# An S4 layer beside a feed-forward on Trainium2: the input transform's stores put on ScalarE's queue, and the last second weight loaded into the buffer of the raw first weights

## The chip, the cores and the metric

The kernel runs on one core of one Trainium2 chip. The metric is the device time of one execution in microseconds (us), lower is better. Three runs of the kernel before give a median of 1121.8.

## The reference, cut to what matters

The input is one sequence of L = 2048 rows with D = 576 channels. It is normalised row by row; the normalised rows go through a state-space layer (S4, a long convolution for each channel) and, in parallel, through a feed-forward with 4608 hidden features; both results are added to the input. Everything is float32.

```python
K = einsum("dn,dnl,dn->dl", C, exp(dt * A * l), dt * B).real    # N = 128 states, l < 2048
y = irfft(rfft(pad(xn)) * rfft(pad(K)))[:2048] + xn * Dskip     # per channel
h = silu(xn @ w1)                                               # 576 -> 4608
return x + y + h @ w2                                           # 4608 -> 576
```

## The kernel before

**Number format.** TensorE is fed in its faster float32 form (fp32r). To keep the precision, every operand is split into a high part and a low part, and every product becomes three matmuls: high by high, high by low, low by high. In names, `h` and `l` at the end mean these parts (`gh`, `gl`; `yh`, `yl`).

**The feed-forward** (`ffn`, `wino_ffn`) carries the program. The 4608 hidden features are 36 tiles of 128 (`NFT`), in blocks of four (`FT`, so `NCH` = 9 blocks). The tokens go in two halves of 1024. For a hidden tile there is a *first weight* (576 x 128 of `w1`) and a *second weight* (128 x 576 of `w2`). In the first half, raw second weights (`w2r`) come in on SyncE's queue (SP) at line 275, ScalarE and VectorE split them (L284), and the split form is also stored to a scratch `dw2` in device memory. In the second half from hidden tile 8 on, a scheme with seven products instead of eight for 2 x 2 blocks of the first product is used (`wino_ffn`). It runs in units n = 4 to 17, of two hidden tiles each, 2n and 2n + 1. A unit needs:

- raw first weights, `load_w1` (SP, tag `w1r`): one tile of 128 x 5 x 256 values for a unit. There are two such buffers, one in the pool `wp` and one in `w1x`, used by units in turn. `prep` then forms the splits and sums of them on ScalarE and VectorE (the last one of a unit's is on L371 in the profile), after which the raw buffer is not read again.
- second weights, already split: `second(n, i)` loads tile 2n + i from `dw2` on GpSimd's queue (POOL, L480) into a ring of five buffers (tag `w2`). It is called from `side_w(3)`, once in each unit, for tile 1 of this unit and tile 0 of the next one. A load can start only when TensorE has read the tile that held the buffer five loads ago for the last time. Tile 35 is the last of all.

The second product is `down`: for each block of 128 tokens and each half of the channels, TensorE sums 24 matmuls or fewer into `po` (L328), and VectorE adds that to the running sum `acc` (L333). The activations are `gf` (silu, on ScalarE, L306), `gh` (L307) and `gl` (VectorE, L308).

**The state-space layer** runs between the steps of the feed-forward. `weave` interleaves the two when the program is written; its tail comes last:

1. `spread`, the input transform: it loads rows of the normalised input (`xr`), splits them (`sp`, L149), TensorE multiplies them with a matrix `s1` into `pu`, ScalarE copies both channel halves to the tile `u1` (L156), and `u1` is stored to the scratch `d1u` (L157). There are 32 such stores of 288 KB, and one buffer `u1` (`u` in the profile). So the next copy has to wait until the store before it has landed.
2. `kgen`, beside it, makes the kernel K with sines on ScalarE and products on VectorE; TensorE sums `z` (L880) from `kt`, and 18 stores of 512 KB take it to the scratch `d1k`, on GpSimd's queue as well (L893), two at a time.
3. `spectral`: 32 steps. SP loads a row block of `d1u` and of `d1k`, TensorE multiplies both with matrices `m` that GpSimd loads (L902), and the product goes back through L997 (`pb`) and ScalarE (`yo`) to the scratch `d2` (GpSimd).
4. the output transform: SP loads `ys` from `d2` (L1004), six row blocks ahead, two DMAs each; `conv` multiplies pairs of them (`py`, L1016). For eight of the sixteen row blocks ScalarE copies the result to `yt` and GpSimd adds it into the output (L172, `out_dram<-yt`, accumulating stores); for the other eight `down` adds the feed-forward's last sum onto it, at the end.

**What sets the order.** The program is built with a scheduler that takes all instructions with their dependencies and a model of their times, and writes one list for each engine (`schedule_with_timeline_sim=True`). Blocks under `high_priority` go first where they can; `behind` keeps an instruction from being put ahead of a given one. So an edit in one place can move instructions elsewhere. [...]

Of the kernel before, what the change touches and what calls it, by code (L numbers as in the profile page):

```python
# [11 lines left out]
F32R = mybir.dt.float32r  # L12
# [5 lines left out]
P = 128  # L18
L = 2048
D = 576  # L20
# [5 lines left out]
NFT = FF // P  # L26
# [15 lines left out]
def kernel(  # L42
# [21 lines left out]
    nc = tc.nc  # L64
    FT = 4
# [38 lines left out]
    wp = ctx.enter_context(tc.tile_pool(name="wp", bufs=2))  # L104
# [33 lines left out]
    def spread(up):  # L138

        s1 = up.tile([P, 2, P], F32R, name="s1", bufs=1)  # L140
        nc.gpsimd.dma_start(s1, cs1)
        for j in range(NJ):
            src = up.tile([P, D], F32, tag="xr", name="xr")
            nc.sync.dma_start(src, dxn[:, j])
            for m in range(2):
                lo, hi = slice(64 * m, 64 * m + 64), slice(64 - 64 * m, 128 - 64 * m)
                u1 = up.tile([P, D], F32, tag="u1", name="u1")
                sp = up.tile([P, D], F32R, tag="sp", name="sp")
                nc.scalar.copy(sp[lo, :], src[lo, :])  # L149
                nc.vector.tensor_sub(sp[hi, :], src[lo, :], sp[lo, :])  # L150
                for h in range(2):
                    hs = slice(h * HD, (h + 1) * HD)
                    pu = pss.tile([P, 512], F32, tag="pss", name="pu")
                    nc.tensor.matmul(pu[:, :HD], s1[:, 0, :], sp[:, hs], start=True, stop=False)
                    nc.tensor.matmul(pu[:, :HD], s1[:, 1, :], sp[:, hs], start=False, stop=True)
                    nc.scalar.copy(u1[:, hs], pu[:, :HD])  # L156
                nc.gpsimd.dma_start(  # L157
                    d1u.rearrange("(p m j) d -> m j p d", m=2, j=NJ)[m, j], u1)
                yield j

# [275 lines left out]
    def wino_ffn(load_w1, prep, WT, first, end, W2, before, down):  # L436

        ps_a = ps1.tile([P, 512], F32, tag="ps1", name="pa")
        ps_c = ps1.tile([P, 512], F32, tag="ps1", name="pc")
        A, A22, S1, S2, S3, S4, x40, x41, d4 = wino["x"]  # L440
        nc.tensor.matmul(ps_a, x40[:, :P], x40, start=True, stop=True)
        G = {}

        def unit(name, n, a):
            h, l = WT[name, n]
            return h[:, a:a + 2], l[:, a:a + 2]

        def prod(dst, w, x, start=False, stop=False):
            (wh, wl), (xh, xl) = w, x
            n = 0  # L450
            for a, v in ((wh, xh), (wh, xl), (wl, xh)):
                for kt in range(2):
                    pins["pe"] = nc.tensor.matmul(dst, a[:, kt], v[:, kt], start=start and n == 0, stop=stop and n == 5,  # L453
                                                  skip_group_check=True).ins
                    n += 1

        def rest(dst, name, n, at, x4, stop=True):
            for i in range(2):
                pins["pe"] = nc.tensor.matmul(dst, WT[name, n][i][:, at], x4, start=False, stop=stop and i == 1,  # L459
                                              skip_group_check=True).ins  # L460

        def gate(src, b, f):
            gf = gp.tile([P, 512], F32, tag="gf", name="gf", bufs=2)
            spare = len(G) % 6 == 5
            gh, gl = ((wino["pool"] if spare else gp).tile([P, 512], F32R, tag=n, name=n) for n in ("gh", "gl"))
            G[b, f] = gh, gl
            with tc.high_priority():
                nc.scalar.activation(gf, src, AF.Silu)
                pins["gh"] = nc.scalar.copy(gh, gf).ins  # L469
                pins["gl"] = nc.vector.tensor_sub(gl, gf, gh).ins  # L470

        def load(n):
            if n < end:
                load_w1(1, n // 2, n % 2 * 2)

        def second(n, i):
            if n < end:
                f = 2 * n + i
                w = wp.tile([P, 2, D], F32R, tag="w2", name="w2", bufs=FT + 1)
                pins["load"] = nc.gpsimd.dma_start(w, dw2[f - WINO_C * FT]).ins  # L480
                W2[1, f // FT, f % FT] = w

        load(first + 1)
        second(first, 0)

        def downs(n):

            if n < first:
                return [lambda jj=jj: down(before, jj) for jj in range(4)]
            b = 1 - n % 2  # L490
            if n == first:
                ns = (n,)
            else:
                ns = (n - 1, n)
            return run_of(b, ns)

        def run_of(b, ns):
            fs = [2 * n + i for n in ns for i in range(2)]
            blk = (1, NCH - 1 if ns[-1] == end - 1 else WINO_C, b)
            return [lambda jj=jj: down(blk, jj, [(G[b, f], W2[1, f // FT, f % FT]) for f in fs]) for jj in range(4)]  # L500

        for n in range(first, end):
            load(n + 2)
            d = downs(n - 1)
            pb = ps2.tile([P, 512], F32, tag="ps2", name="pb2")
            f5 = wino["pool"].tile([P, 512], F32, tag="f5", name="f5", bufs=1)
            units = {k: unit(*k) for k in (("c1", n, 0), ("c1", n, 2), ("t13", n, 0), ("t13", n, 2),
                                           ("t24", n, 0), ("t24", n, 2), ("c2", n, 0))}

            def p1():  # L510
                prod(pb, units["c1", n, 0], A[0], start=True)
                with tc.high_priority():
                    nc.scalar.copy(ps_a, pb)

            def p5():
                prod(ps_c, units["t13", n, 0], S1, start=True)
                rest(ps_c, "c2", n, 2, x41)
                with tc.high_priority():
                    nc.scalar.copy(f5, ps_c)

            def p6():
                prod(pb, units["t24", n, 0], S2)
                with tc.high_priority():
                    nc.vector.tensor_add(ps_c, pb, f5)

            def p7():
                prod(pb, units["t13", n, 2], S3)
                with tc.high_priority():
                    nc.vector.tensor_add(f5, pb, f5)

            def c11():
                prod(ps_a, units["c1", n, 2], A[1])
                rest(ps_a, "c1", n, 4, x40)
                gate(ps_a, 1, 2 * n)

            def c12():
                prod(ps_c, units["c2", n, 0], S4)
                rest(ps_c, "c2", n, 2, d4)
                gate(ps_c, 1, 2 * n + 1)

            def c2x():
                gate(f5, 0, 2 * n + 1)
                prod(pb, units["t24", n, 2], A22)
                gate(pb, 0, 2 * n)

            def c1x():
                c12()
                c11()

            def side_w(k):  # L550
                if k == 1:
                    prep(n + 1, "c2")
                elif k == 2:
                    prep(n + 1, "c1")
                    prep(n + 1, "sums")
                elif k == 3:
                    second(n, 1)
                    second(n + 1, 0)

            if n == first:  # L560
                order = ((p1, 0), (c11, 1), (2,), (p5, p6, 3), (p7,))
                ends = c12, c2x
            else:
                order = ((p1, p5), (0,), (p6, 1), (p7, 2), (3,))
                ends = (c1x, c2x) if n % 2 == 0 else (c2x, c1x)
            for steps in order:
                for f in steps:
                    if callable(f):
                        f()
                    else:  # L570
                        d[f]()
                        side_w(f)
                yield 0
            rest(pb, "c1", n, 4, x41, stop=False)
            for k, f in enumerate(ends):
                f()
                prep(n + 1, ("t13", "t24")[k])
                yield 0
        b = 1 - (end - 1) % 2
        for f in run_of(b, (end - 2, end - 1)):  # L580
            f()
            yield 0
        for k, f in enumerate(run_of(1 - b, (end - 1,))):
            f()
            if k % 2:
                yield 0
# [579 lines left out]
```

## Time and profile before

| | before |
|---|---|
| median of three runs | 1121.8 us (1121.65 to 1125.08) |
| the profiled execution's own time | 1124.72 us |
| its span, first to last instruction | 1123.0 us |
| granted TensorE clock, mean | 0.995 |
| TensorE (PE) busy | 1094.8 us, 97% |
| VectorE (DVE) busy | 939.7 us, 84% |
| ScalarE (ACT) busy | 737.7 us, 66% |
| GpSimd (POOL) busy | 170.1 us, 15% |
| moved by DMA | 173.68 MB, mean 155 GB/s |

All moments and durations below are of the one profiled execution and are counted from the start of its span. A row of instructions reads: start, duration, engine, line, operation, result <- operands, shape, count, and in brackets the idle time of the engine ahead of it with what ended that. A row of waits reads: engine, tile and line, <- what released it: total, count, longest. A row of a window (A:B) reads: its length, then busy time and count of PE, PEld (weight loads), DVE, ACT, POOL, then the granted clock, the share of the DMA engines, and GB/s. A row of DMA issues gives the size of each transfer and the us from issue to landing. Buffer numbers are left out of names unless a text says otherwise.

### The profile page before, as it was taken

What the parts mean: (1) busy time and instruction counts of PE and PEld (TensorE: products, weight loads), DVE (VectorE), ACT (ScalarE), POOL (GpSimd) and SP (SyncE); (2) the same over time, 40 slices, a digit from 0 to 9 for tenths busy, and PEclk for the clock granted to TensorE, in tenths of its full rate; (3) what the DMA queues carried; (4) which work ended last, traced back from release to release, by engine and by line L of the source; (5) the groups of instructions that cost most, each with busy time, mean ns of one, the idle gap of its engine ahead of it and who ended that gap; (6) DMA issues with size and microseconds to landing.
All of it is one profiled execution on the core that took longest, in us unless ns stands there. A gap on an engine that the chain in (4) does not pass through costs nothing.

```text
span 1123.0 us, 23098 instructions
## 1 busy us (share of the span) xinstructions
PE 1094.8 (97%) x9101; PEld 988.9 (88%) x9101; DVE 939.7 (84%) x1597; ACT 737.7 (66%) x1321; POOL 170.1 (15%) x262
## 2 busy tenths in 40 slices
PE   6999899999899999999999999999999999999997
PEld 5998789898788889898899898999999999999786
DVE  6699888899899999989999978989888788886322
ACT  4665556777676767766776646877778787875320
POOL 1022100101010101010522012112111211210220
PEclk9999989999999999999999999999999999999999
DMA  9456532525344444447773334555555655554994
GB/s 271 141 163 202 163 121 70 160 82 157 122 126 121 139 152 124 157 92 251 231 192 101 95 71 142 188 174 153 171 177 175 178 164 158 175 158 114 230 222 104
DMA packets 90445, 173.68 MB, mean 155 GB/s; under 512 B 14768, under 2 KB 53696, under 8 KB 89696
## 3 DMA queue, kind: packets, MB, share of 16 engines
q1 hardware_dynamic: 63184, 97.32, 29.3%
q0 software_dynamic: 26480, 73.11, 23.4%
q10 hardware_dynamic: 672, 1.77, 0.7%
q8 instruction: 72, 1.18, 0.4%
q14 instruction: 37, 0.30, 0.1%
HBM read 109.64 MB, written 62.60 MB: 153 GB/s over the span
## 4 chain that ended last, share of the span: by engine, by line
PE 78%; DVE 6%; DMA 6%; issue 4%; ACT 3%; POOL 1%; SPq 0%; POOLq 0%; DVEq 0%; ACTq 0%
PE po L328 34%; PE ph L298 15%; PE pb L453 7%; PE pc L453 3%; PE kp L865 2%; PE pb L997 2%; PE pu L997 2%; PE pk L997 2%; DMA d1u<-u 2%; PE pa L453 2%; PE ph L300 1%; PE ph L299 1%; PE z L880 1%; PE pc L459 1%; DMA w1r<-in_B_w_dram 1%
## 5 line engine op out<-in xcount | busy, mean ns | idle before, releaser
L328 PE MATMUL po<-w,gh 128*128 128x288 f32 x2304 | 477.2, 297 | 8.2 <-DVE acc L333 3.2
L328 PEld LDWEIGHTS po<-w,gh 128*128 128x128 f32 x2304 | 375.8, 188 | 25.5 <-issue 6.0
L328 PE MATMUL po<-w,gl 128*128 128x288 f32 x1152 | 334.8, 296 | 0.6 <-DVE gl L308 0.6
L328 PEld LDWEIGHTS po<-w,gl 128*128 128x128 f32 x1152 | 215.5, 188 | 3.0 <-DVE gl L308 0.9
L333 DVE TENSOR_TENSOR acc<-po,acc 128x288 f32<-128x288 f32 x296 | 129.5, 450 | 65.8 <-PE po L328 64.6
L298 PE MATMUL ph<-xh,w1h 128*128 128x512 f32 (+1 forms) x368 | 100.3, 391 | 2.4 <-ACT w1h L266 1.3
L298 PE MATMUL ph<-xl,w1h 128*128 128x512 f32 (+1 forms) x368 | 100.4, 387 | 0.0
L298 PE MATMUL ph<-xh,w1l 128*128 128x512 f32 (+1 forms) x368 | 98.1, 383 | 0.0
L306 ACT ACTIVATE gf<-ph 128x512 f32<-128x512 f32 (+1 forms) x92 | 53.2, 578 | 51.0 <-PE ph L300 35.8
L298 PEld LDWEIGHTS ph<-xl,w1h 128*128 128x128 f32 x368 | 67.4, 192 | 12.1
L298 PEld LDWEIGHTS ph<-xh,w1h 128*128 128x128 f32 x368 | 66.4, 194 | 13.1 <-ACT w1h L266 1.6
L298 PEld LDWEIGHTS ph<-xh,w1l 128*128 128x128 f32 x368 | 66.2, 188 | 11.6
L902 POOL DMA_DIRECT2D m<-in_cm_dram x64 | 33.9, 532 | 216.2 <-PE pu L997 135.4
L308 DVE TENSOR_TENSOR gl<-gf,gh 128x512 fp32r<-128x512 f32 (+1 forms) x92 | 60.7, 661 | 4.0 <-ACT gh L307 3.8
L826 ACT ACTIVATE c<-th 128x1040 f32<-128x1040 f32 x36 | 38.7, 1074 | 36.2 <-DVE th L825 36.1
L307 ACT CAST gh<-gf 128x512 fp32r<-128x512 f32 (+1 forms) x92 | 55.4, 604 | 8.2 <-PE po L328 6.8
L157 POOL DMA_DIRECT2D d1u<-u x32 | 17.8, 557 | 275.4 <-ACT u L156 275.4
L824 ACT ACTIVATE c<-th,magic 128x1040 f32<-128x1040 f32 x36 | 42.0, 1166 | 23.7 <-DVE C L845 19.3
L470 DVE TENSOR_TENSOR gl<-gf,gh 128x512 fp32r<-128x512 f32 x56 | 37.8, 688 | 20.7 <-ACT gh L469 20.3
L844 DVE TENSOR_TENSOR S<-th,C 128x1024 f32<-128x1024 f32 x36 | 43.9, 1220 | 13.4 <-ACT th L827 13.3
L893 POOL DMA_DIRECT2D d1k<-stage x18 | 29.6, 1647 | 151.8 <-ACT u L156 99.9
L825 DVE SCALAR_TENSOR_TENSOR th<-c,th 128x1040 f32<-128x1040 f32 x36 | 44.4, 1234 | 3.1 <-ACT c L824 3.0
(273 smaller groups left out, 2419.3 us busy)
## 6 DMA issues: line engine op xcount, KB each, us to landing
w1r<-in_B_w_dram SPq DMA_DIRECT2D x35, 512.0 KB, 4.0
dw<-w SPq DMA_DIRECT2D x28, 576.0 KB, 4.2
w<-dw POOLq DMA_DIRECT2D x28, 576.0 KB, 5.5
w2r<-in_B_w_dram SPq DMA_DIRECT2D x44, 288.0 KB, 5.0
d1u<-u POOLq DMA_DIRECT2D x32, 288.0 KB, 3.7
d1k<-stage POOLq DMA_DIRECT2D x18, 512.0 KB, 8.7
ul<-d1u SPq DMA_DIRECT2D x32, 288.0 KB, 2.9
kl<-d1k SPq DMA_DIRECT2D x32, 288.0 KB, 3.6
```

The source lines that it names most:

```text
L298: nc.tensor.matmul(ph, w[:, kt, :], v[:, kt, a:e], start=n + kt == 0, stop=False)
L306: nc.scalar.activation(gf, ph, AF.Silu)
L307: pins["gh"] = nc.scalar.copy(gh, gf).ins
L308: pins["gl"] = nc.vector.tensor_sub(gl, gf, gh).ins
L328: pins["pe"] = nc.tensor.matmul(po[:, :HD], gs[g][:, js], ws[:, w, hs], start=n == 0 and j not in begun, stop=n == 3 * len(terms) - 1, ski ...
L333: nc.vector.tensor_add(acc[j][:, hs], po[:, :HD], acc[j][:, hs])
L453: pins["pe"] = nc.tensor.matmul(dst, a[:, kt], v[:, kt], start=start and n == 0, stop=stop and n == 5, skip_group_check=True).ins
L824: nc.scalar.activation(c65, th, AF.Identity, bias=magic)
L825: nc.vector.scalar_tensor_tensor(th, c65, MAGIC, th, op0=ALU.subtract, op1=ALU.subtract)
L826: nc.scalar.activation(c65, th, AF.Abs)
L844: nc.vector.tensor_mul(ov3, t[:, :, 0:64].rearrange("n d (x y) -> n d x y", y=32), mv3)
L997: nc.tensor.matmul(dst, st, mv[:, hs], start=n == 0, stop=n == 3 * len(terms) - 1)
```

## The change

Two edits.

*First*, `spread` issues its 32 stores of `u1` with `nc.scalar.dma_start` instead of `nc.gpsimd.dma_start`. Data, size, buffer and destination stay.

*Second*, the load of the last second weight, tile 35 of 36 (f = `NFT` - 1), no longer takes a buffer of the ring `w2`. It goes into the buffer that held the raw first weights of an even unit (tag `w1r` in `wp`; 10 x 128 of its values, of which 2 x 576 are used). Unit 16 is the last to use that buffer for raw weights. The call comes at `side_w(3)` of unit 16 (`n == end - 2`) instead of unit 17, right after those for tiles 33 and 34. The call of unit 17 then finds tile 35 in the table `W2` and does nothing. GpSimd still issues it.

```diff
@@ spread
-                nc.gpsimd.dma_start(
+                nc.scalar.dma_start(
                     d1u.rearrange("(p m j) d -> m j p d", m=2, j=NJ)[m, j], u1)
@@ wino_ffn
         def second(n, i):
-            if n < end:
-                f = 2 * n + i
-                w = wp.tile([P, 2, D], F32R, tag="w2", name="w2", bufs=FT + 1)
+            f = 2 * n + i
+            if n < end and (1, f // FT, f % FT) not in W2:
+                if f == NFT - 1:
+                    w = wp.tile([P, 10 * P], F32R, tag="w1r", name="w2", bufs=1)
+                    w = w[:, :2 * D].rearrange("p (k d) -> p k d", k=2)
+                else:
+                    w = wp.tile([P, 2, D], F32R, tag="w2", name="w2", bufs=FT + 1)
                 pins["load"] = nc.gpsimd.dma_start(w, dw2[f - WINO_C * FT]).ins
                 W2[1, f // FT, f % FT] = w
@@ side_w
                 elif k == 3:
                     second(n, 1)
                     second(n + 1, 0)
+                    if n == end - 2:
+                        second(n + 1, 1)
```

The edit adds six lines, so a line number of the program before that lies behind `second` is six higher in the program after (L997 becomes L1003); `second`'s own DMA goes from L480 to L484.

**GpSimd, the last second weights.** This is the end of GpSimd's list before, from the last stores of the spectral step on. The names `w_...` are second weights: w_12839 is tile 31, w_12841 tile 32, w_13125 tile 33, w_13127 tile 34, and w_13399 tile 35.

```order
L952 DMA d_59<-yo 128x576 x3
L480 DMA w_12839<-dw_63 128x1152
L480 DMA w_12841<-dw_63 128x1152
L172 DMA out_dram<-yt 32x1152 x8
L480 DMA w_13125<-dw_63 128x1152
L480 DMA w_13127<-dw_63 128x1152
L172 DMA out_dram<-yt 32x1152 x8
L480 DMA w_13399<-dw_63 128x1152
```

And after, where tile 35 is w_13129:

```order
L958 DMA d_59<-yo 128x576 x3
L484 DMA w_12839<-dw_63 128x1152
L484 DMA w_12841<-dw_63 128x1152
L484 DMA w_13129<-dw_63 128x1152
L172 DMA out_dram<-yt 32x1152 x8
L484 DMA w_13125<-dw_63 128x1152
L172 DMA out_dram<-yt 32x1152 x4
L484 DMA w_13127<-dw_63 128x1152
L172 DMA out_dram<-yt 32x1152 x4
```

Tile 35 has moved from the end to right behind tile 32, ahead of all the accumulating stores, and four of these stores now stand between tiles 33 and 34.

**TensorE, the last product of the spectral step.** The place is the second product of unit 15's activations, whose first reader of second weight 31 is still to come; m_12092 is the last matrix of the spectral step, and w_12086, w_12381, w_12383 and w_12601 are second weights 26 to 29. Before:

```order
L328 MATMUL po<-w_12383,gl 128x288
L997 MATMUL pb<-yh,m_12092 128x288 x2
L328 MATMUL po<-w_12601,gh 128x288 x2
L997 MATMUL pb<-yl,m_12092 128x288
L997 MATMUL pb<-yh,m_12092 128x288
L997 MATMUL pb<-yl,m_12092 128x288
L997 MATMUL pb<-yh,m_12092 128x288
L328 MATMUL po<-w_12601,gl 128x288
L328 MATMUL po<-w_12086,gh 128x288 x2
```

After:

```order
L328 MATMUL po<-w_12086,gh 128x288 x2
L328 MATMUL po<-w_12086,gl 128x288
L328 MATMUL po<-w_12381,gh 128x288
L1003 MATMUL pb<-yh,m_12092 128x288 x2
L328 MATMUL po<-w_12381,gh 128x288
L328 MATMUL po<-w_12381,gl 128x288
L1003 MATMUL pb<-yl,m_12092 128x288
L1003 MATMUL pb<-yh,m_12092 128x288
L1003 MATMUL pb<-yl,m_12092 128x288
L1003 MATMUL pb<-yh,m_12092 128x288
L328 MATMUL po<-w_12383,gh 128x288 x2
L328 MATMUL po<-w_12383,gl 128x288
```

The six matmuls of the product have moved back against the second product: behind their last one, 40 matmuls followed before up to the last one that reads w_12086, and 9 follow now. The buffer of w_12086 (tile 26) is the one that tile 31 goes to.

**ScalarE, one of the 32 stores.** The place is in the input transform, at the tile u_3100, whose store goes out right behind a pair of `d1k` stores. The names c and th are tiles of the sines, and w_3225 is a split second weight. Before:

```order
L824 ACTIVATE c_3327<-th,magic 128x1040
L156 COPY u_3100<-pu 128x288
L149 CAST sp<-xr 64x576
L284 CAST w_3225<-w2r 128x576
L306 ACTIVATE gf<-ph 128x512
L826 ACTIVATE c_3327<-th 128x1040
L827 ACTIVATE th<-th 128x1040
L828 ACTIVATE c_3327<-c_3327,halfpi 128x1040
L306 ACTIVATE gf<-ph 128x512
L156 COPY u_3212<-pu 128x288 x2
```

After:

```order
L830 ACTIVATE c_3327<-th,magic 128x1040
L156 COPY u_3100<-pu 128x288
L149 CAST sp<-xr 64x576
L284 CAST w_3225<-w2r 128x576
L157 DMA d1u<-u_3100 128x576
L306 ACTIVATE gf<-ph 128x512
L832 ACTIVATE c_3327<-th 128x1040
L833 ACTIVATE th<-th 128x1040
L834 ACTIVATE c_3327<-c_3327,halfpi 128x1040
L306 ACTIVATE gf<-ph 128x512
L156 COPY u_3212<-pu 128x288 x2
```

The store does not stand directly behind the copy that it waits for, but two casts later; behind it come a `gf` and two sines, and then the copy of the next tile into the same buffer.

## The prediction

> **What bounds the kernel now.** I read the page's busy times and chain, then TensorE's waits, then the windows in which they fall.
>
> ```profile
> PE 1094.8 (97%) x9101; PEld 988.9 (88%) x9101; DVE 939.7 (84%) x1597; ACT 737.7 (66%) x1321; POOL 170.1 (15%) x262
> PE 78%; DVE 6%; DMA 6%; issue 4%; ACT 3%; POOL 1%; SPq 0%; POOLq 0%; DVEq 0%; ACTq 0%
> PE pt L122 <- DVE xn L190: 8.9, 1, 8.9
> PE po L328 <- DVE acc L333: 3.2, 2, 2.0
> PE z L880 <- ACT kt L872: 2.2, 3, 1.2
> PE po L328 <- DMA w<-dw: 2.0, 1, 2.0
> 280.80:308.80 28.00, 24.80 (x279) 22.35 (x279) 24.65 (x37) 17.33 (x29) 1.64 (x3) 1.00 0.38 122
> 1038.80:1066.80 28.00, 28.00 (x228) 22.08 (x228) 10.81 (x22) 10.78 (x25) 8.39 (x12) 1.00 1.00 230
> ```
>
> TensorE is busy for 97% of the span, and 78% of the chain that ended last lies on it. The change removes no matmul, so it can win only TensorE's idle time, or time at a low clock. The first wait (8.9 us) is the load at the start, which the change leaves alone. Two others are within its reach: the one for a second weight (2.0), and the idle 3.2 us (28.00 less 24.80) from 280.8 on. From 1038.8 on the DMA engines are full (share 1.00, 230 GB/s) while TensorE never idles: a later transfer is felt there only where it has no slack.
>
> **Part one of the change: the last second weight.** The rows are GpSimd's loads of second weights (w<-dw) and one of its stores, the last load's flight, TensorE around it, and the window behind it (the column 0.50 is the granted clock).
>
> ```profile
> 1033.33 1.09 POOL L480 DMA_DIRECT2D w<-dw  x2 [5.42 <-PE po L328]
> 1062.20 2.27 POOL L480 DMA_DIRECT2D w<-dw  x2
> 1065.90 3.16 POOL L172 DMA_DIRECT2D out_dram<-yt  x4 [1.43 <-ACT yt L966]
> 1090.24 8.11 DMA w<-dw
> 1096.16 0.29 PE L328 MATMUL po<-w,gh 128*128 128x288 f32 x1
> 1098.49 0.51 PE L328 MATMUL po<-w,gh 128*128 128x288 f32 x2 [2.04 <-DMA w<-dw]
> 1077.01 3.18 PE po L328 x24
> 1098.90:1102.30 3.40, 3.40 (x24) 2.89 (x30) 1.77 (x4) 0.00 (x0) 0.00 (x0) 0.50 0.00 1
> 1037.81 1.15 DVE L371 TENSOR_TENSOR w1l<-w1r,w1h 128x512 fp32r<-128x512 f32 x2
> ```
>
> Load 35 goes out at 1090.24, when TensorE has let go of its buffer, and flies 8.11 us. Between the matmuls at 1096.16 and 1098.49 lie 2.33 us, where such matmuls follow each other every 0.13 (3.18 for 24): **2.2 us** lost. Behind it the clock is half for 3.40 us: another **1.7 us**.
>
> In the new order load 35 stands right behind load 32. It waits for the last reading of unit 16's raw weights, by 1037.81 plus 1.15, and is needed 59 us later: even the longest flight here leaves it far ahead. Both terms go. What is late next? Load 34 now stands behind four stores (a row of four takes 3.16 us from 1065.90), so it leaves at about 1069 instead of 1063; its first use is beside load 35's, near 1093, so 24 us are left, and it costs nothing.
>
> The price lies elsewhere. The scheduler has also moved the last product of the spectral step, whose stored result SP waits for before it loads ys for the output transform:
>
> ```profile
> 1026.27 0.29 PE L997 MATMUL pb<-yh,m 128*128 128x288 f32 x1
> 1029.98 18.99 SPq L1004 DMA_DIRECT2D ys<-d  x16
> 1043.32 1.20 PE L1016 MATMUL py<-ys,s 64*32 64x288 f32 x24
> w<-dw POOLq DMA_DIRECT2D x2, 576.0 KB, 9.8
> ys<-d SPq DMA_DIRECT2D x1, 288.0 KB, 12.4
> w<-dw POOLq DMA_DIRECT2D x1, 576.0 KB, 9.6
> 1071.84 0.50 PE L328 MATMUL po<-w,gh 128*128 128x288 f32 x2
> ```
>
> (The three DMA rows are the windows 1033.3 to 1033.9, twice, and 1062.1 to 1062.5; last column: us to landing.) Before, that product ran at 1026.27. By the new order only 9 matmuls lie between it and the last reading of second weight 26, which releases load 31 at 1033.3; so it runs about 1.2 us (9 x 0.13) before that, near 1031.6: 5.3 later, and ys starts near 1035.3. The first py product stands where it stood, at 1043.3. It now has 8 us for the four ys loads of its pair. At 230 GB/s a ys load (288 KB) takes 1.3 us and a second weight 2.6, and loads 31 and 32 now lead: 2 x 2.6 + 4 x 1.3 = 10.4 us of transfers from 1033.3, ending at 1043.7, plus a flight of some 2. The ends are no wait and 5.2 (both weights wholly in front, nothing overlapped); I take **+1.0**, since the first product needs only half of the pair.
>
> Load 33 is next. It left at 1062.20, landed 9.6 later at 1071.8, and TensorE used it at 1071.84: no slack. The train of loads before it now begins 3.3 us later (1033.3, not 1030.0) and is longer by load 35's 2.6: up to 5.9 late. Against that, GpSimd's loads overtake SP's here (9.8 beside 12.4 for issues in the same 0.6 us), so the delay falls mostly on ys loads with time to spare. I take 0 for load 33; 5.9 is a rival's.
>
> **Part two: 32 stores from GpSimd's queue to ScalarE's.** ScalarE's waits for these stores, the worst of them, SP's issues beside it, and what TensorE lost:
>
> ```profile
> ACT u L156 <- DMA d1u<-u: 14.1, 6, 4.8
> 275.01 12.28 DMA d1u<-u
> 275.18 0.68 ACT L284 CAST w<-w2r 128x576 fp32r<-128x576 f32 x1
> 277.59 0.60 ACT L306 ACTIVATE gf<-ph 128x512 f32<-128x512 f32 x1 [1.73 <-PE ph L300]
> 287.37 0.70 ACT L156 COPY u<-pu 128x288 f32<-128x288 f32 x2 [4.83 <-DMA d1u<-u]
> 293.18 1.16 PE L880 MATMUL z<-f,kt 64*128 64x128 f32 x16 [1.24 <-ACT kt L872]
> 301.79 0.53 PE L328 MATMUL po<-w,gh 128*128 128x288 f32 x2 [1.96 <-DVE acc L333]
> 275.47 1.38 SPq L275 DMA_DIRECT2D w2r<-in_B_w_dram  x1
> 280.96 2.28 SPq L275 DMA_DIRECT2D w2r<-in_B_w_dram  x1
> w2r<-in_B_w_dram SPq DMA_DIRECT2D x1, 288.0 KB, 11.5
> w2r<-in_B_w_dram SPq DMA_DIRECT2D x1, 288.0 KB, 3.6
> L165 ACTq DMA_DIRECT2D acc<-in_A_u_dram x4: 370/438/443, 0.7 to 2.1; - x4
> L893 POOL DMA_DIRECT2D d1k<-stage x18 | 29.6, 1647 | 151.8 <-ACT u L156 99.9
> ```
>
> (The two w2r rows with KB are the loads of 275.47 and 331.43.) Two large stores d1k (18 in all, so 9 bursts) go out at 271.5 and 273.1; the d1u store behind them takes 12.28 us, so ScalarE cannot refill the single buffer u and waits 4.83. TensorE then idles 1.24 and 1.96, 3.2 us for 4.83: 0.66 per us.
>
> *What a new queue wins.* In the new order the store stands behind the cast of w, so it leaves near 275.9. A transfer of the same 288 KB on SP's queue at 275.47 took 11.5 us; so the store lands near 287.4, where it landed at 287.3. Gain 0. The other end is the load of 331.43, half a us into its burst: 3.6 us, and the whole 3.2 us are won. I take 0, as 275.47 is the nearer row. [...]
>
> *What the issue costs.* ScalarE's four own DMA issues took 0.44 us. 32 x 0.44 = 14 us, but each stands behind a cast of 0.6 us or longer, under which it can run, and ScalarE is 66% busy. In a burst an issue can stick: 1.38 and 2.28 us on SP. Queued behind it are gf (for TensorE's next products) and the two sines that VectorE waits for. Ends: 0, if the idle 1.73 us that follow at 277.59 cover it, and 9 x 2.28 x 0.66 = 13.6 us. I take one burst without that cover, 1.38 x 0.66 = **+0.9**. GpSimd loses its 32 issues, which no row here waits for.
>
> **The sum.** -2.2 - 1.7 + 1.0 + 0 + 0.9 = -2.0 us on a span of 1123.0 (an execution of 1124.7). That execution is 2.9 us above the median of the runs; the difference is put on the median: 1121.8 - 2.0 = **1119.8**. A measurement of this kernel can tell about 0.3%, 3.4 us, from no change.
>
> **Rivals.**
> *The stores land early and the wait at the end goes*: -3.9 - 3.2 = -7.1, 1114.7; without the new ys wait and issue cost but with no gain on the stores, -3.9, 1117.9. For it: 3.6 us at 331.43. Against: 11.5 at 275.47. [...] Chance 0.30.
> *Load 33 comes late* (slower): 5.9 us of wait and a half clock of 1.7 again: -2.0 + 5.9 + 1.7 = +5.6, 1127.4. For it: no slack at 1071.84, DMA share 1.00. Against: GpSimd's loads overtake. It decides from a wait of 3.7 us. Chance 0.17.
> *ScalarE sticks in its issues* (slower): +13.6 for +0.9 gives +10.7, 1132.5; it decides from 9.5 us of blocking, 1.06 per burst (6.3 / 0.66). In the new order 19 of the 32 stores also wait for a counter shared with SP's transfers, which adds to it. Against: the idle time behind the issue. Chance 0.13.
> *It does nothing*: something else holds TensorE at 1096. Against: the row names the load alone. 1121.8, chance 0.02.
>
> **The numbers.** Forecast 0.38 (its own range 1118.4 to 1123.0). Faster by over 0.3%: 0.30. Within: 0.38 + 0.02 = 0.40. Slower: 0.17 + 0.13 = 0.30. The range 1114.0 to 1129.0 holds the first rival and the second, and leaves out most of the third and a little below the first.
>
> **What would show it.** Right: no wait of po on w<-dw near 1096, no half clock behind it; ScalarE still waits about 14 us on d1u; ys starts near 1035; py waits 0 to 2 us. Wrong: ScalarE's waits on d1u near 0 (first rival); po waiting on w<-dw near 1071 (second); DMA issues over 1 us on ScalarE and more waits on acc and kt (third).

## The result and the profile after

The changed kernel takes **1119.67 us** (median of 14 runs, 1116.19 to 1121.6); the kernel before, run 14 times in turn with it, takes 1122.73 (1119.62 to 1127.89). The ratio is 0.9966, with a 95% interval of 0.9952 to 0.998: 3.8 us of 1122.7, just past the 0.3% that can be told. The forecast was 1119.8, 2.0 us faster and within 0.3%. The number came out near, but the parts of the sum did not; they are taken apart below. One of the twelve executions of experiment 3 took 1190.6 us, where the others took 1115.6 to 1120.07, and is left out of its ratio.

The page of the profiled execution after (1118.54 us, span 1116.8):

```profile
PE 1091.8 (98%) x9101; PEld 987.3 (88%) x9101; DVE 940.6 (84%) x1597; ACT 737.0 (66%) x1321; POOL 152.6 (14%) x230
```

The same number of matmuls in 6.2 us less of span. That is more than the runs give: this execution lies 1.1 us below its kernel's median, and the profiled one of before 2.0 above its own. So single profiles place a change here, but do not size it.

**Part one, the load of tile 35.** GpSimd's loads of tiles 35, 33 and 34 in the timeline after, and the first products with tiles 33 and 35:

```profile
1035.36 0.53 POOL L484 DMA_DIRECT2D w<-dw  x1 [4.33 <-DVE w1l L371]
1060.73 0.59 POOL L484 DMA_DIRECT2D w<-dw  x1 [2.26 <-PE po L328]
1064.65 0.59 POOL L484 DMA_DIRECT2D w<-dw  x1 [0.16 <-issue]
...
1068.47 0.42 PE L328 MATMUL po<-w,gh 128*128 128x288 f32 x2
1089.77 0.42 PE L328 MATMUL po<-w,gh 128*128 128x288 f32 x2
```

The DMA view of the same trace, from 1060.6 to 1060.9, load 33 (last column us to landing):

```profile
w<-dw POOLq DMA_DIRECT2D x1, 576.0 KB, 7.2
```

And the windows view for the end:

```profile
1085.00:1112.00 27.00, 26.88 (x288) 23.46 (x286) 9.90 (x21) 3.80 (x7) 0.00 (x0) 1.00 0.52 122
```

Load 35 leaves at 1035.36, when VectorE has read the raw weights for the last time, and its tile is first used at 1089.77. TensorE has no wait there, and the granted clock in the end window is 1.00 (the third number from the right). Load 33 lands at 1067.9 (1060.73 + 7.2) and is used at 1068.47: 0.5 us to spare, where the second rival saw it late.

**The price of the new order.** SP's loads of ys and the second group of the output transform's products, in the timeline after:

```profile
1031.89 11.58 SPq L1010 DMA_DIRECT2D ys<-d  x12
1042.92 0.72 PE L1022 MATMUL py<-ys,s 64*32 64x288 f32 x16 [1.20 <-DMA ys<-d]
```

These products take plain float32: one of 288 columns lasts 403 ns in the middle, one of `po` with as many columns in fp32r 294 (the tile view of `po` after).

Two of TensorE's waits that were not there before:

```profile
PE py L1022 <- DMA ys<-d: 1.2, 1, 1.2
PE pk L1003 <- DVE kb L933: 0.7, 1, 0.7
```

The wait for ys is there, 1.2 us, as forecast (+1.0). The second row was not forecast: in the spectral step, the first product now waits for VectorE.

**Part two, the stores.** The burst that the prediction looked at, on GpSimd (d1k), ScalarE and SP, in the timeline after:

```profile
270.83 3.24 POOL L899 DMA_DIRECT2D d1k<-stage  x2 [50.29 <-ACT stage L894]
274.21 0.33 ACTq L157 DMA_DIRECT2D d1u<-u  x1
274.53 0.32 SPq L288 DMA_DIRECT2D dw<-w  x1
273.80 0.38 ACT L156 COPY u<-pu 128x288 f32<-128x288 f32 x1
274.08 0.68 ACT L149 CAST sp<-xr 64x576 fp32r<-64x576 f32 x1
274.65 0.68 ACT L284 CAST w<-w2r 128x576 fp32r<-128x576 f32 x1
283.20 0.70 ACT L156 COPY u<-pu 128x288 f32<-128x288 f32 x2 [1.19 <-DMA d1u<-u]
```

The same copy in the timeline of before, whose store left at 275.01:

```profile
274.33 0.38 ACT L156 COPY u<-pu 128x288 f32<-128x288 f32 x1
```

The DMA view of after from 272.40 to 275.00, that store's row:

```profile
d1u<-u ACTq DMA_DIRECT2D x1, 288.0 KB, 8.9
```

ScalarE's waits for d1u, the window behind the burst, and the 32 issues by line (ns, least, median and most), each from its own view of after:

```profile
ACT u L156 <- DMA d1u<-u: 5.8, 3, 4.2
```
```profile
280.80:308.80 28.00, 27.80 (x298) 25.21 (x297) 25.37 (x39) 19.43 (x32) 0.00 (x0) 1.00 0.41 134
```
```profile
L157 ACTq DMA_DIRECT2D d1u<-u x32: 326/326/358, 180.9 to 640.1; - x32
```

The store flies 8.9 us instead of 12.28, and ScalarE waits 1.19 us for it instead of 4.83. The store leaves 0.03 us behind the end of its copy (274.18), where on GpSimd it left 0.30 behind (274.71 to 275.01). TensorE idles 0.2 us in the window instead of 3.2. And no issue on ScalarE sticks: 358 ns is the most of all 32.

### The profile page after: what moved, and what is told of

Same layout as the page of the kernel before. It is cut to its first block, busy times and chain, and to the rows that moved or that the text cites. A ratio compares the mean times of both kernels' runs of the same rounds, so it can differ in the third digit from the quotient of the medians.

```text
span 1116.8 us, 23071 instructions
## 1 busy us (share of the span) xinstructions
PE 1091.8 (98%) x9101; PEld 987.3 (88%) x9101; DVE 940.6 (84%) x1597; ACT 737.0 (66%) x1321; POOL 152.6 (14%) x230
## 3 DMA queue, kind: packets, MB, share of 16 engines
q0 software_dynamic: 23920, 63.67, 20.8%
## 4 chain that ended last, share of the span: by engine, by line
PE 76%; DVE 8%; DMA 7%; ACT 4%; issue 4%; POOL 0%; SPq 0%; ACTq 0%; POOLq 0%; DVEq 0%
PE po L328 32%; PE ph L298 17%; PE pb L453 6%; PE pc L453 3%; PE kp L871 3%; PE pb L1003 2%; PE pk L1003 2%; PE pu L1003 2%; PE z L886 1%; PE ph L299 1%; PE ph L300 1%; PE pa L453 1%; DMA w1r<-in_B_w_dram 1%; DMA kl<-d1k 1%; DVE acc L333 1%
## 5 line engine op out<-in xcount | busy, mean ns | idle before, releaser
L814 DVE TENSOR_TENSOR th<-vt,fT 128x1040 f32<-128x1040 f32 x36 | 44.4, 1237 | 0.1
```

The source lines that it names most:

```text
L814: nc.vector.tensor_mul(split(th), row(vt[:, 0:65], 65), col(fT, i, 65))
```

## The experiments

**How the stages are sized.** The kernels' profiles are compared by an excess worked out from the starts of all matmuls: for each pair of neighbours, start to start less the median for that line and shape, summed over three stages that end at the same matmuls in every kernel: the input transform, the spectral step, and the rest. The time ahead of the transform is alike in all kernels, and there the excess varied from 12.4 to 16.6 us. So about 2 us either way in one execution is chance. Only differences between kernels are read from this table, since another choice of the usual pace shifts a column for all kernels alike.

| kernel (profiles) | TensorE's order | ratio, 95% interval | transform | spectral | last stage |
|---|---|---|---|---|---|
| before (1) | old | 1 | 11.5 | 0.9 | 13.5 |
| load alone (2) | old | 0.998 [0.9959, 1.0]; 0.9982 [0.9967, 0.9997] | 8.1; 12.9 | 2.3; 1.0 | 9.7; 9.7 |
| stores alone (1) | new | 0.9979 [0.9961, 0.9998] | 5.3 | 3.4 | 11.6 |
| the change (3) | new | 0.9966 [0.9952, 0.998]; 0.9972 [0.9951, 0.9994]; 0.9964 [0.9947, 0.9982] | 5.8; 7.3; 5.6 | 4.0; 4.3; 3.7 | 9.9; 13.2; 9.3 |
| load behind 34 (1) | new | 0.9965 [0.9949, 0.9982] | 7.4 | 4.1 | 9.5 |
| stores on SP (1) | old | 0.9944 [0.9925, 0.9964] | 9.0 | 0.8 | 9.7 |
| burst stores on ScalarE (2) | old | 0.9945 [0.9923, 0.9966]; 0.9943 [0.9918, 0.9967] | 7.1; 7.6 | 2.1; 1.9 | 10.0; 9.7 |
| burst ScalarE, rest SP (1) | old | 0.995 [0.9932, 0.9968] | 7.8 | 2.8 | 10.0 |

"Old" and "new" are the written orders of TensorE: the old one is that of the kernel before (but for up to ten places at the end), the new one that of the changed kernel. It is the 32 stores on ScalarE, not the load, that bring the new order.

One stretch needs no such reckoning. From the first product of the transform until 302 us in the profile of before, TensorE runs the same 1221 matmuls in the same order in every kernel of the table; two of the eight bursts lie in it. From its first to its last matmul the stretch lasts 123.3 to 124.4 us in the three profiles with all stores on GpSimd (before and twice the load alone), and 121.4 to 122.8 us in the nine others. So the stores of the first two bursts win about 2 us by leaving GpSimd's queue, with nothing moved on TensorE.

**1. The load alone** (the change with its store line put back):

```diff
-                nc.scalar.dma_start(
+                nc.gpsimd.dma_start(
                     d1u.rearrange("(p m j) d -> m j p d", m=2, j=NJ)[m, j], u1)
```

> Only the load of tile 35 is moved; the 32 stores stay on GpSimd. In the written order all engines but GpSimd stand as before, up to ten matmul places at the end. Forecast's terms: the wait at 1096 (2.2 us) and the half clock behind it (1.7) go, the spectral step does not move, so ys has no new wait: 3.9 us faster, ratio 0.9965; ScalarE still waits about 14 us on d1u. Rival (load 33 late): the 576 KB of tile 35 delay load 33, which had no slack, by up to 2.6 us: a wait of po on w<-dw near 1071 of 1 to 3 us, and a ratio of 0.998 to 1.000. Second rival (the half clock is not tied to that wait): 2.2 us, 0.998.

The median is 1119.87 beside 1123.77 of before. TensorE has no wait at the end, as the forecast's terms have it, and ScalarE still waits 10.1 us for d1u, where about 14 were expected. The ratio gives 2.2 us, not 3.9: it is the second rival's number, though its interval, 0 to 4.6 us, holds both.

**2. The stores alone** (the kernel before with `nc.scalar.dma_start` in `spread`, and nothing else):

> Only the 32 stores go to ScalarE; tile 35 stays where it was. The written order of TensorE, VectorE and ScalarE is word for word that of the changed kernel. If the stores win what the profile of the changed kernel suggests (3.2 us at 280 to 309, 2 to 3 more in later bursts) less a ys wait of 1.2: 3 to 5 us faster, ratio 0.996 to 0.997, with the wait for tile 35 near 1091 still there. If the forecast's terms hold in the median (stores 0, issues +0.9, ys +1.0): 1.9 us slower, ratio 1.002.

Median 1120.84. The first product with tile 35 in its timeline:

```profile
1090.63 0.50 PE L328 MATMUL po<-w,gh 128*128 128x288 f32 x2 [2.14 <-DMA w<-dw]
```

And the window behind it (the column ahead of the last two is the granted clock):

```profile
1090.60:1101.00 10.40, 10.37 (x100) 9.66 (x101) 2.75 (x6) 0.00 (x0) 0.00 (x0) 1.00 0.62 138
```

The wait for tile 35 is as long as before (2.14 us), yet the granted clock behind it stays 1.00: the half clock does not belong to that wait in every execution. The load's 2.2 us in experiment 1 fits the wait alone. The stores win 2.4 us by the ratio; the forecast's terms had them lose 1.9.

**3. The stores on SP** (`nc.sync.dma_start`, load early):

> As the changed kernel, but the 32 stores go to SyncE's queue. The written order of TensorE is then that of the kernel with the load alone, and ScalarE issues nothing. If it is enough that the stores leave the queue in which the d1k stores stand ahead of them: landing in a burst 8 to 10 us instead of 12.3, ScalarE's waits on d1u 6 us or less, and as fast as the changed kernel or up to 1 us faster (no ys wait), ratio 0.995 to 0.997. If SyncE's list holds the stores back (each stands behind loads that may stick 1.4 to 2.3 us in their issue), waits on d1u stay at 10 us or more and the ratio is that of the load alone, about 0.9965 or above.

Median 1117.89, 2.6 us below the changed kernel on the same chip (1120.48). ScalarE waits 9.7 us on d1u, not 6 or less, and the transform's excess, 9.0 us, is above that of every kernel in the table with stores on ScalarE. But TensorE has the old order, the spectral step's excess is 0.8 us and nothing waits for ys.

**4. The change again.**

> The changed kernel once more, beside the parts on the same chip. By the two profiles, 6.2 us faster (ratio 0.9945); by the medians of 14 runs each, 0.9966. If the profile of before was an execution with about 2 us of chance on top, its span here is 1115 to 1119 and the ratio near 0.9966; the parts should add up to it within 1.5 us.

Median 1120.48. Its profiled execution took 1125.21 us, and shows what the new order can cost. The products of the output transform in its timeline:

```profile
1044.58 0.81 PE L1022 MATMUL py<-ys,s 64*32 64x288 f32 x16 [0.75 <-DMA ys<-d]
1048.03 1.14 PE L1022 MATMUL py<-ys,s 64*32 64x288 f32 x16 [2.04 <-DMA ys<-d]
```

The window behind the second wait, and then its waits:

```profile
1048.20:1051.60 3.40, 3.40 (x26) 2.52 (x14) 0.00 (x0) 0.70 (x2) 1.40 (x3) 0.50 1.09 223
```
```profile
PE py L1022 <- DMA ys<-d: 2.8, 2, 2.0
PE pk L1003 <- DVE kb L933: 0.9, 1, 0.9
```

Here ys costs 2.8 us of waiting and 3.40 us at half clock, which lose another 1.7: 4.5 in all.

**5. Load 35 behind load 34** (the buffer of the raw weights kept, the call left where it was before):

```diff
-                pins["load"] = nc.gpsimd.dma_start(w, dw2[f - WINO_C * FT]).ins
+                with behind(pins["load"] if f == NFT - 1 else None):
+                    pins["load"] = nc.gpsimd.dma_start(w, dw2[f - WINO_C * FT]).ins
...
-                    if n == end - 2:
-                        second(n + 1, 1)
```

> As the changed kernel (all stores on ScalarE, tile 35 in the buffer of raw weights), but load 35 is put behind load 34 in GpSimd's list, and nothing else moves on any engine. If the wait for ys near 1041 to 1046 (1.2 and 2.8 us in the two profiles of the changed kernel, the second with 3.4 us of half clock behind it) comes from load 35's 576 KB beside the ys loads: py waits under 0.5 us, the last stage's excess falls from 9.9 and 13.2 us to about 9.7, ratio 0.995, no wait for w<-dw near 1090 (20 us of slack). If ys is late only because the spectral step's last product was moved: py still waits 1 to 3 us, ratio as for the changed kernel, 0.997.

Median 1119.2. The load left at 1063.82 and nothing waited for it; but TensorE's waits still have one for ys:

```profile
PE py L1021 <- DMA ys<-d: 0.7, 1, 0.7
```

0.7 us, where the changed kernel had 1.2, 2.8 and 0.6 in its three profiles, and the stores alone 0.5. So a wait for ys remains without load 35 ahead of it. It is there in all five profiles of the new order and in none of the old, so it comes with the moved spectral product; whether load 35 lengthens it cannot be told from these. The ratio, 0.9965, is that of the changed kernel.

**6 and 10. Eight stores on ScalarE**, those right behind a pair of d1k stores; the other 24 on GpSimd; load early. TensorE keeps the old order:

```diff
-                nc.scalar.dma_start(
+                (nc.scalar if j % 2 == 0 and m == 1 else nc.gpsimd).dma_start(
```

> Load 35 early; of the 32 stores only the 8 that stand right behind a pair of d1k stores go to ScalarE, the other 24 stay on GpSimd. TensorE's written order is that of the kernel with the load alone. If the gain of the stores is that of leaving the queue in which two d1k stores stand ahead: ScalarE waits 6 us or less on d1u, excess of the transform stage 5 to 7 us (10 on GpSimd), the spectral stage keeps its excess of 1 us and ys has no wait: ratio 0.993 to 0.995. If what was won in the transform came from the new order instead: waits on d1u about 10 us, excess 8 to 11, ratio that of the load alone, 0.9965 to 0.998.

> Eight burst stores on ScalarE, the others on GpSimd, load 35 early, TensorE's order that of the kernel with the load alone. If the queue by itself wins 1 to 3 us in the transform: 1 to 3 us below the load alone, ratio 0.994 to 0.996. If the first runs were chance: level with the load alone.

Medians 1117.69 and 1117.28. ScalarE's waits on d1u are 9.1 and 5.6 us, where 6 or less were expected. **9**, the load alone beside the second of them:

> The load alone, again, beside the three that follow. From its first runs: 2.2 us faster by the ratio (0.998), 3.9 by the medians. If its two terms (2.2 and 1.7) are right: ratio 0.9965, excess of the last stage 9.7 us again, ScalarE's waits on d1u 10 to 14 us, every d1u store of a burst landing behind its d1k pair.

Median 1121.35; the last stage's excess is 9.7 us again, but the ratio is 0.9982, not the 0.9965 expected. The load alone over the transform, by windows:

```profile
178.00:640.00 462.00, 455.20 (x4687) 408.50 (x4687) 427.67 (x622) 325.37 (x499) 62.33 (x86) 1.00 0.48 142
```

The same window with the eight stores on ScalarE (experiment 10):

```profile
178.00:640.00 462.00, 459.31 (x4723) 412.33 (x4722) 433.84 (x632) 328.53 (x505) 58.55 (x78) 1.00 0.49 144
```

ScalarE's waits on d1u are 13.2 us in the first and 5.6 in the second. With TensorE's order the same, TensorE idles 6.8 us (462.00 less 455.20) and 2.7 us. So moving eight stores to another queue wins without the new order. By the medians it is 4.1 us, and the two intervals only touch (0.9967 and 0.9967).

**11. The change a third time**, on the same chip:

> The changed kernel beside the two above. If the new written order costs 2.4 us in the spectral stage and 0.2 to 3.5 us at the wait for ys, against 1.5 won in the transform beyond the burst stores: 1 to 4 us above the kernel with the eight burst stores, ratio 0.997; excess of the spectral stage 3.5 to 4.5 us against 1 to 2 us. If the order costs nothing: level with it.

Median 1119.22, 1.9 us above the kernel with the eight stores. Its spectral excess is 3.7 us against 1.9. The two intervals overlap, so these two runs alone do not show the new order to be slower; but all four runs of kernels with the old order and the stores off GpSimd's burst lie at 0.9943 to 0.995, and all four of the new order with the load early at 0.9964 to 0.9972.

**12. Eight on ScalarE, 24 on SP:**

> Eight burst stores on ScalarE, the other 24 on SyncE, load 35 early, the same order on TensorE. A candidate for the fastest: if GpSimd's own issuing (0.54 us a store, 1.65 a d1k store) also delayed the stores, 0.5 to 1 us below the kernel with the eight burst stores, ratio 0.993 to 0.994; else level with it, 0.9945.

Median 1118.21, against 1117.28 with the other 24 on GpSimd: nothing more was won by emptying GpSimd's queue.

**7 and 8. The d1k stores on ScalarE**, with d1u on GpSimd (7) and with both on ScalarE (8):

```diff
-                        nc.gpsimd.dma_start(kv[gp_, :, :, d0:d0 + NRUN * CH], stage[gp_ * 64:(gp_ + 1) * 64])
+                        nc.scalar.dma_start(kv[gp_, :, :, d0:d0 + NRUN * CH], stage[gp_ * 64:(gp_ + 1) * 64])
```

> Load 35 early, d1u stores on GpSimd as before, but the 18 large d1k stores on ScalarE's queue: the two kinds are on different queues, the other way round. If separate queues are what counts: d1u stores behind a burst land in 9 us or less and ScalarE waits 6 us or less on d1u. If ScalarE's queue is faster by itself for d1u: landing 12 us as before, waits 10 us or more. The time is not decisive: the written order in the transform stage differs.

> Load 35 early, d1u and d1k stores both on ScalarE's queue, one behind the other as they were on GpSimd's. If separate queues are what counts: landing of the d1u stores in bursts back to 12 us, waits on d1u 10 us or more. If it is the hardware queue of ScalarE: landing 9 us or less, waits 6 us or less. The time is not decisive for the same reason.

Medians 1128.92 (ratio 1.0056 [1.0035, 1.0077]) and 1144.43 (1.0195 [1.017, 1.022]). Experiment 8's burst on ScalarE, in its timeline:

```profile
271.55 4.24 ACTq L899 DMA_DIRECT2D d1k<-stage  x1
275.89 0.60 ACT L306 ACTIVATE gf<-ph 128x512 f32<-128x512 f32 x1 [4.24 <-DVE pw L805]
278.52 2.26 ACTq L157 DMA_DIRECT2D d1u<-u  x1
```

All its d1k issues on ScalarE (ns, least, median and most):

```profile
L899 ACTq DMA_DIRECT2D d1k<-stage x18: 597/1796/5865, 215.8 to 686.3; - x18
```

ScalarE's own queue in the DMA view of after, and then of experiment 8 (packets, MB, share of the engines):

```profile
q10 hardware_dynamic: 5280, 11.21, 3.0%
q10 hardware_dynamic: 79296, 20.65, 8.4%
```

The 18 d1k stores make 74016 packets more there, some 4100 each. On GpSimd's queue (q0) the same stores are 2592 packets, 144 each: it has 23920 packets in after and 21328 in experiment 8.

Neither experiment told the queue theories apart by the flight of d1u: ScalarE itself stood 4.24 us in a d1k issue, so the d1u store left 4.5 to 8 us behind the pair instead of about 2, and flew 4.8 (7) and 5.0 us (8) in this burst, beside a median of 9.0 of its d1k pair in both. The order of landing can still be read in the other kernels. In all eight bursts (behind the ninth pair of d1k no d1u store follows) of before and in both profiles of the load alone, where both kinds share GpSimd's queue, d1u lands 0.7 to 1.6 us *behind* the second d1k store. In the changed kernel's first profile, on separate queues, it lands 0.9 to 5.1 us *ahead* of it in seven of eight bursts (in the eighth it already left ahead of the second d1k store), and in both profiles of the eight stores on ScalarE 0.7 to 5.3 us ahead in the same seven. Experiments 7 and 8 add nothing to this: leaving that late, d1u lands behind in seven of eight bursts on separate queues (7) and in all eight on a shared one (8). So leaving GpSimd's queue let the store overtake; whether it is the d1k stores ahead in that queue, or something else of that queue, was not separated. Experiment 8 also shows what the third rival feared, though with other stores: ScalarE sticks in d1k issues for up to 5.9 us, and the kernel is 21 us slower.

## Why the prediction was right in its number and wrong in its parts

From the table's means over profiles, the change adds up so: transform 10.8 (three profiles with all stores on GpSimd) to 6.3 (five of the new order), **-4.5**; spectral step 1.7 (seven, old order) to 3.9 (five), **+2.2**; the wait for tile 35, **-2.2**, with the half clock up to 1.7 more where it comes; ys and what follows in the last stage, 10.8 (three) less 9.7, **+1.1**. That is -3.4; the three ratios of the change say -3.1 to -4.0. With about 2 us of chance in each profile, a term is known to 1 or 2 us, so the close agreement of the sum is partly chance.

- *Load 35: -2.2 and -1.7.* The wait was right to a tenth (2.14 where it was left in), and load 35 early had slack. The half clock was taken as fixed, from one execution. Experiment 2 has the wait without it, and the load alone wins 2.0 to 2.2 us by the ratios. The granted clocks of all executions say the same: the load alone has a mean of 0.9970 beside 0.9960 of before on one chip, and 0.9953 beside 0.9959 on the other, which over the span of some 1120 us is about 1 us won and half a us lost. So most of this 1.7 was not there in the mean.
- *ys: +1.0.* Right in size, and for the reason given: the product moved back, ys left after loads 31 and 32. It started at 1031.89, not near 1035, since everything ahead had come some 3 us earlier. The flight of some 2 us in its reckoning is about what the 72 KB stores out_dram<-acc on SP took in before, 2.1 us. Its spread (0.6 to 2.8 us of waiting, with a half clock behind the longest) lies within the bounds 0 and 5.2.
- *Load 33: 0.* Right, with 0.5 us to spare.
- *Stores: gain 0.* The step that failed, with two faults in it. The stand-in for the new flight was the w2r load of 275.47 with 11.5 us. But that load stood second on its queue. The first on SP's queue in the same burst was the store dw<-w, twice as large, and it flew 7.1 us; this is the window of before from 275.04 to 275.20 in the DMA view:

```profile
dw<-w SPq DMA_DIRECT2D x1, 576.0 KB, 7.1
```

That row, also a store and first on its queue, was the nearer one to the store's 8.9 us, though it is no fixed figure either: the same dw<-w store flew 9.6 us in after. And the store did not wait for the casts ahead of it in ScalarE's list. It left at 274.21, when its tile was ready, while the cast of sp still ran and 0.44 us ahead of the cast of w, not behind that cast, where the prediction put it (near 275.9). So here a DMA left before an instruction that stands ahead of it in its engine's list. The first rival thus had this part right, and the marks of neither came out whole: ScalarE waits 5.8, 5.6 and 3.3 us on d1u, not 14 and not 0. The new queue saved 0.3 us from the end of the copy to the issue (0.30 to 0.03) and 3.4 of flight (12.28 to 8.9).
- *Issues on ScalarE: +0.9.* No sign of it: 32 issues of 0.33 us, none stuck; the 19 waits for a counter on the store's line took 17 ns each.
- *Not seen at all: +2.2 in the spectral step.* The prediction read the new order at the one place where it touched ys. But from 302 us on, 3935 of TensorE's 9101 matmuls have another line, tile or shape at their place in the trace than before. In every profile of the new order the spectral product pk waits for VectorE's `kb` (0.7 to 1.3 us), and in none of the old. That is about half of the 2.2; where the rest lies was not settled.

So 0 for -4.5, -1.7 for a half clock that is not always there, +0.9 for issues that cost nothing to be seen, and 0 for +2.2 nearly cancelled. That the forecast came within 0.2 us of the measured median is luck: errors of up to 4.5 us cancelled, and the median of three runs that it started from lay 0.9 us below that of 14. The gain itself was forecast at 2.0 us and measured at 3.8 by the ratio.

## What to carry to other kernels

A store that stood behind large stores on its issuer's queue was sped up here by another queue: it flew 8.9 us instead of 12.28 in the burst at 274. Where a kernel has such a store, try it. Estimate its new flight from the first transfer on a separate queue in the same burst rather than from one queued second, and allow a range: that first transfer took 7.1 us in one profile here and 9.6 in another. Try moving only the stores that stand in the bursts: eight on ScalarE came out at ratios of 0.9943 and 0.9945, all 32 at 0.9964 to 0.9972. The 32 also brought a new order on TensorE; all 32 on SP, which kept the old order, came out at 0.9944. And look through the whole reordered list for products that now come before their operands, not only where a known wait is near.

## What the runs showed that was not expected

Whether a half clock came behind a short wait was not decided here by the length of the wait. Among the pauses of TensorE of 2.0 to 2.3 us past its usual pace, after the start-up and in all profiles, three of ten were followed by 3.4 us at half clock (before at 1096, experiment 4 at 1046, experiment 9 at 465). Seven were not (before at 300, experiment 2 at 1088, experiment 4 at 289, experiment 7 at 298, experiment 8 at 299 and 338, experiment 9 at 300). What does decide it was not shown.

The same DMA was another thing on another issuer: a 512 KB d1k store held GpSimd 1.62 to 1.68 us each time, and ScalarE 0.6 to 5.9 us, while a 288 KB d1u store in the changed kernel held ScalarE 0.33 us.
